# Last query group in two halves, and one operand's transposing loads held back until another has landed, in a two-attention kernel

## The chip, the cores and the metric

The kernel runs on one core of a Trainium2 chip. The metric is the device time of one execution in microseconds (us). Most executions of one kernel agree within 0.3%; an execution more than 1.5% above the fastest of its kernel counts as slow and is left out of the ratios. A profile is one further look at an execution: its span runs from the first to the last instruction and is some 2 us shorter than the device time. TensorE's granted clock is given as a share of full speed.

## The reference, cut to what matters

Two attentions, A and B, read two inputs of 2048 rows by 448 columns, and their outputs stand side by side.

```python
# A: 16 query heads of 28 columns share one key and one value head, full softmax
q = (x @ wq) as 16 heads;  k = x @ wk;  v = x @ wv
p = softmax(q k^T * 28 ** -0.5);  outA = (p v, heads joined) @ wo
# B: 16 heads; each query sees 8 keys at distances 0, 2, .. 14
q, k, v = x @ wqkv;  attn = softmax(q . k[pos - 2 w] * 28 ** -0.5, masked where pos < 2 w)
outB = (sum_w attn * v[pos - 2 w]) @ wo
```

A's scores are 16 heads x 2048 x 2048 exponentials, and they set the time. B is laid between them.

## The kernel before

A Python generator registers operations, each with what it reads (`R`), what it writes (`W`), an estimated duration and a priority `pr`. A scheduler derives the waits and lays all operations in one fixed order per engine. On the chip each engine then works through its own order: an operation that waits holds up everything behind it.

The loads. `xst` is a staging tile for A's first 512 rows; TensorE transposes them. All other rows come by transposing loads on SyncE's queue, A's (`xT_A`, 12 loads) and B's (`xT_B`, 16).

```python
a("act", 0.5, one(lambda e: e.dma_start(out=g.xst[:, :, :], in_=g.A_x[0, 0:512, :]...)),
  W=["xst"], dsem="i_xa0", land=3.2, pr=-21)
...
a("sp", 1.05, one(lambda e, c=c, t=t: e.dma_start(out=g.xT_A[...], in_=g.A_x[...], transpose=True)),
  R=["xst"], W=[("xT", c, t)], ..., pr=-20 + c)          # R is used here as "not before this has landed"
...
a("sp", 1.05, one(lambda e, c=c, t=t: e.dma_start(out=g.xT_B[...], in_=g.B_x[...], transpose=True)),
  W=[("xT_B", c, t)], ..., pr=-16 + c)
...
a("gp", 1.5, ..., W=["wqv"], dsem="i_wbv", land=5, pr=-7, ninc=2)   # B's value weights, GpSimd's queue
...
a("sp", 0.6, one(lambda e: e.dma_start(out=g.v_dram[0:PAD, :], in_=g.Vst[0:PAD, 0, :])),
  R=[("Vst", 0)], W=[("vd", -1)], dsem="i_vz", ..., pr=3, rel=4)     # 14 rows of zeros, end of the queue
```

B's first product. VectorE multiplies queries and keys of B into a tile that lies in the same memory as `xst` (the profile calls both `stage`), so the first block has to wait for everyone who still reads `xst`:

```python
op = a("dve", t_dve_2x(1024), ..., W=[("prodT", t)], pr=pr, rel=T)
if k == 0:
    op.deps.update(g.s.rd.get("xst", ()))     # all registered readers of xst
```

The score loop takes 512 queries of one of four head groups at a time ("group", 16 in all). In it ScalarE takes exponentials of three or two banks at once, VectorE takes 4 or 6 single banks of a group and none of the first (`OFF_AT`), and TensorE accumulates P times V in one bank. The last group's result is transposed and normalised in two column halves, one after the other, after the last exponential (`hv = 2`).

## Time and profile before

| before | |
|---|---|
| median of 3 runs | 461.0 us (460.56 to 461.21) |
| span of the profiled run | 459.2 us |
| to the first exponential / first start to last start / last end to end | 11.29 / 439.67 / 7.48 us |
| last `xT_B` load landed | 42.6 us |
| first multiply of B started | 53.1 us |

The middle number is start to start, so it leaves out the last exponential itself (0.76 us here).

### The profile page before, as it was taken

What the parts mean: (1) busy time and instruction counts of PE and PEld (TensorE: products, weight loads), DVE (VectorE), ACT (ScalarE), POOL (GpSimd) and SP (SyncE); (2) the same over time, 40 slices, a digit from 0 to 9 for tenths busy, and PEclk for the clock granted to TensorE, in tenths of its full rate; (3) what the DMA queues carried; (4) which work ended last, traced back from release to release, by engine and by line L of the source; (5) the groups of instructions that cost most, each with busy time, mean ns of one, the idle gap of its engine ahead of it and who ended that gap; (6) DMA issues with size and microseconds to landing.
All of it is one profiled execution on the core that took longest, in us unless ns stands there. A gap on an engine that the chain in (4) does not pass through costs nothing.

```text
span 459.2 us, 8717 instructions
## 1 busy us (share of the span) xinstructions
PE 427.7 (93%) x3682; PEld 163.6 (36%) x3682; DVE 380.7 (83%) x622; ACT 444.9 (97%) x430; POOL 9.4 (2%) x29
## 2 busy tenths in 40 slices
PE   8999999999999989999899999899899998989997
PEld 3333232323533324234353342224244342325343
DVE  6556889988798898989688889998988969889883
ACT  3999999999999999999999999999999999999994
POOL 7000000000000000000000000000000000000000
PEclk9999999999999999999999999999999999999999
DMA  7774303002201002020220120002022221214001
GB/s 152 128 162 95 109 27 100 1 1 90 92 15 40 19 10 82 20 81 22 81 91 30 44 83 18 0 13 92 0 97 92 70 78 30 72 31 142 10 1 61
DMA packets 42102, 27.34 MB, mean 60 GB/s; under 512 B 17474, under 2 KB 41904, under 8 KB 42064
## 3 DMA queue, kind: packets, MB, share of 16 engines
q1 hardware_dynamic: 40464, 25.28, 19.6%
q0 software_dynamic: 304, 0.73, 0.6%
q10 hardware_dynamic: 1296, 0.79, 0.5%
q8 instruction: 29, 0.48, 0.4%
q14 instruction: 9, 0.07, 0.1%
HBM read 17.60 MB, written 5.52 MB: 50 GB/s over the span
## 4 chain that ended last, share of the span: by engine, by line
ACT 86%; PE 11%; DVE 1%; DMA 1%; issue 0%
ACT expT L806 85%; PE ps L789 2%; PE ps L1079 2%; PE ps L850 2%; PE ps L787 1%; DMA stage<-in_A_x_dram 1%; PE ps L978 1%; PE ps L1086 1%; PE ps L937 1%; ACT e_t L1054 0%; PE ps L654 0%; PE ps L738 0%; PE ps L1028 0%; PE ps L434 0%; PE ps L993 0%
## 5 line engine op out<-in xcount | busy, mean ns | idle before, releaser
L806 ACT ACTIVATE expT<-ps 128x1024 bf16<-128x1024 f32 (+1 forms) x410 | 438.8, 1209 | 2.1 <-PE ps L789 1.9
L789 PE MATMUL ps<-qT,kT 32*128 32x512 bf16 x824 | 122.3, 385 | 11.6 <-ACT expT L806 9.3
L850 PE MATMUL ps<-expT,v_aug 128*32 128x512 bf16 x958 | 94.8, 389 | 1.0 <-ACT expT L806 1.0
L787 PE MATMUL ps<-qT,kz 128*128 128x512 bf16 x200 | 59.6, 383 | 9.9 <-ACT expT L806 9.4
L789 PEld LDWEIGHTS ps<-qT,kT 32*128 32x128 bf16 x824 | 30.1, 91 | 91.7 <-ACT expT L806 68.4
L883 DVE TENSOR_SCALAR d_x<-ps 128x512 f32<-128x512 f32 x66 | 45.4, 688 | 17.9 <-PE ps L789 16.8
L850 PEld LDWEIGHTS ps<-expT,v_aug 128*32 128x32 bf16 x958 | 24.3, 93 | 62.0 <-issue 55.4
L1073 DVE TENSOR_TENSOR prod<-Vsh,a_n 128x896 bf16<-128x896 bf16 x64 | 37.5, 614 | 7.9 <-PE ps L1079 7.9
L1019 DVE TENSOR_TENSOR stage<-qTB,kTB 112x1024 bf16<-112x1024 bf16 x64 | 42.3, 674 | 1.8 <-PE ps L1028 1.7
L1079 PE MATMUL ps<-ident,prod 128*112 128x128 bf16 x512 | 41.8, 224 | 0.0
L894 DVE SCALAR_TENSOR_TENSOR d_u<-d_u,d_x 128x1024 f32<-128x1024 f32 x33 | 40.1, 1215 | 0.1
L896 DVE SCALAR_TENSOR_TENSOR dexp<-d_u,d_x 128x1024 int16<-128x1024 f32 x33 | 40.0, 1213 | 0.1
L892 DVE SCALAR_TENSOR_TENSOR d_u<-d_x 128x1024 f32<-128x1024 uint16 x33 | 39.9, 1209 | 0.2
L1079 PEld LDWEIGHTS ps<-ident,prod 128*112 128x112 bf16 x512 | 34.2, 130 | 14.7 <-issue 10.9
L978 PE MATMUL ps<-xT_B,wqkv 128*128 128x512 bf16 x128 | 38.9, 383 | 0.0
L787 PEld LDWEIGHTS ps<-qT,kz 128*128 128x128 bf16 x200 | 12.2, 97 | 31.1 <-ACT expT L806 28.9
L1028 PEld LDWEIGHTS ps<-ones,stage 112*128 112x128 bf16 x512 | 18.5, 96 | 7.8 <-issue 4.8
L1028 PE MATMUL ps<-ones,stage 112*128 112x4 bf16 x512 | 21.2, 167 | 0.0
L738 PE MATMUL ps<-xT_A,wq 128*128 128x512 bf16 x64 | 19.8, 384 | 0.1
L1086 PE MATMUL ps<-wo_B,oT 112*128 112x448 bf16 x64 | 18.1, 357 | 0.0
L993 PE MATMUL ps<-wqv,xT_B 128*128 128x448 bf16 x64 | 17.5, 356 | 0.0
L913 DVE STREAM_TRANSPOSE PV_T<-ps 128x512 f32<-128x512 f32 (+1 forms) x17 | 11.4, 676 | 6.7 <-PE ps L850 6.5
(103 smaller groups left out, 303.3 us busy)
## 6 DMA issues: line engine op xcount, KB each, us to landing
Vsh<-v_scratch SPq DMA_DIRECT2D x16, 896.0 KB, 4.6
v_scratch<-Vst SPq DMA_DIRECT2D x16, 112.0 KB, 1.7
out_dram<-outB SPq DMA_DIRECT2D x16, 112.0 KB, 1.7
out_dram<-outA SPq DMA_DIRECT2D x14, 112.0 KB, 1.7
wqkv<-in_B_wqkv_dram SPq DMA_DIRECT2D x1, 672.0 KB, 5.4
stage<-in_A_x_dram ACTq DMA_DIRECT2D x1, 448.0 KB, 4.0
wo_B<-in_B_wo_dram SPq DMA_DIRECT2D x4, 98.0 KB
wo<-in_A_wo_dram SPq DMA_DIRECT2D x4, 98.0 KB
```

The costliest lines, as they stand in the source:

```text
L787: r = e.matmul(g.bank(b0 + i), g.kz[:, j, 128 * tb:128 * tb + 128], g.qT[:, sc % 2, t, :], start=True, stop=True)
L789: r = e.matmul(g.bank(b0 + i), g.kT[32 * j:32 * j + 32, 128 * tb:128 * tb + 128], g.qT[32 * j:32 * j + 32, sc % 2, t, :], start=True, stop ...
L806: x = a("act", t_exp(w), lambda e, b0=b0, w=w, n=n: e.activation(g.expT[:, n % ERING, 0:w], g.ps[:, 512 * b0:512 * b0 + w], ACT.Exp, scale ...
L850: x = e.matmul(g.bank(PVBANK, p0=32 * j, p1=32 * j + 32), g.v_aug[:, w, tb, :], src, start=first, stop=last, tile_position=(0, 32 * j))
L883: o = a("dve", t_dve_ps(512), lambda e: e.tensor_scalar(out=xx[:, 512 * h:512 * h + 512], in0=g.bank(bank), scalar1=-128.0 * A2, scalar2=1 ...
L892: a("dve", t_dve_1x(1024), lambda e: e.scalar_tensor_tensor(out=u, in0=lo, scalar=EP * F, in1=lo, op0=ALU.add, op1=ALU.mult), R=di, W=["d_ ...
L894: a("dve", t_dve_1x(1024), lambda e: e.scalar_tensor_tensor(out=v, in0=u, scalar=EQ * F * F, in1=lo, op0=ALU.add, op1=ALU.mult), R=["d_u"] ...
L896: a("dve", t_dve_1x(1024), lambda e: e.scalar_tensor_tensor(out=out, in0=v, scalar=EL / F ** 3, in1=xx, op0=ALU.mult, op1=ALU.subtract), R ...
L978: a("pe", t_mm(512), lambda e, u=u, t=t, kt=kt, w=w: e.matmul(g.bank(u.bank), g.wqkv[:, kt, w * D + KC * t:w * D + KC * t + 128], g.xT_B[: ...
L1019: op = a("dve", t_dve_2x(1024), lambda e, t=t, qv=qv, kv=kv: e.tensor_tensor(out=g.prodT[0:KC, t, :, :], in0=qv, in1=kv, op=ALU.mult), R=R ...
L1028: r = e.matmul(g.bank(u.bank, 128).rearrange("p (h w) -> p h w", w=WIN)[:, 4 * t:4 * t + 4, w], g.prodT[0:KC, t, w, :], g.ones4[:, :], sta ...
L1079: a("pe", 0.056, lambda e, u=u, t=t, w=w: e.matmul(g.bank(u.bank, 128, 128 * t, p1=KC), g.prod2[:, w, KC * t:KC * t + KC], g.ident[:, :], ...
```

## The change

Its intent: the last group is worked in two halves of 256 queries, so that the first half is normalised and projected while the second is still being scored, and only half remains after the last exponential. B's transposing loads wait for A's first rows, so that these land alone. Two warming matmuls are added. Six score banks on VectorE in three groups, which the change's label also names, are in the kernel before as well. Not shown below: the second half evicts no bank to VectorE, some priorities of A's projections change, and the scheduler charges for one more kind of mode switch on TensorE. These too can move the static order. The core of the diff, with cuts:

```diff
-TAILB = (0, 1, 2, 4)
-WARM = 7
+TAILB = (4, 0)
+WARM = 9
 OFF_AT.update({q: (0, 2, 3, 5, 7, 8) for q in (5, 9, 13)})
+OFF_AT[15] = (0, 2, 3, 5)
...
-  ... in_=g.B_x[...], transpose=True)), W=[("xT_B", c, t)], dsem=f"i_xb{c}.{t}", land=4.5, pr=-16 + c)
+  ... in_=g.B_x[...], transpose=True)), R=["xst"], W=[("xT_B", c, t)], dsem=f"i_xb{c}.{t}", land=4.5, pr=-16 + c)
...
+    def parts(self, u):
+        if u[:2] == (3, 3):       # last group: two key blocks of 256 queries in one bank
+            return [(2 * (u[2] % 8) + i, 256 * (u[2] // 8), 256) for i in range(2)]
+        return [(u[2], 0, 512)]
...
-    def a_quad_end(self, sc, t):
+    def a_quad_end(self, sc, t, hf=None):     # called once for each half of the last group
-        hv = 2 if last else 1
-        for hf in range(hv):
...
-        for s4 in range(4):
+        for s4 in range(4) if hf is None else (2 * hf, 2 * hf + 1):
```

More of the change, by code (lines that the diff above doesn't have):

```diff
@@ L284, in run @@
                     o.dense += 512 * o.fill
-                if o.tiled and not mode:
+                if o.tiled and (not mode or o.fill):
                     o.dur += self.MODE
@@ L609, in loads @@
                     out=g.xT_B[:, t, 512 * c:512 * c + 512], in_=g.B_x[0, 512 * c:512 * c + 512, XB0[t]:XB0[t] + 128],
-                    transpose=True)), W=[("xT_B", c, t)], dsem=f"i_xb{c}.{t}", land=4.5, pr=-16 + c)
+                    transpose=True)), R=["xst"], W=[("xT_B", c, t)], dsem=f"i_xb{c}.{t}", land=4.5, pr=-16 + c)
         a("sp", 1.2, lambda e: [
@@ L758, in a_q, with key @@
               R=["qadd"], W=[("qT", par, t)], use=u, pr=pr if first else -1)
+    def key(self, u):
+        return (3, 3, u[2] // 8) if u[:2] == (3, 3) else u[:2]
+    def parts(self, u):
+        if u[:2] == (3, 3):
+            return [(2 * (u[2] % 8) + i, 256 * (u[2] // 8), 256) for i in range(2)]
+        return [(u[2], 0, 512)]
     def a_loop(self):
@@ L764, in a_loop @@
         g.last_exp, g.pvs, g.evacs = {}, {}, []
-        quads = {(sc, t): [[] for _ in range(4)] for sc in range(4) for t in range(4)}
+        quads = {g.key(u): [[] for _ in range(4)] for u in units}
         dqs = {k: [[] for _ in range(4)] for k in quads}
@@ L784, in qk @@
                     e.matmul(g.bank(b0), g.warm[:, 0:128], g.warm[:, :], start=True, stop=True)
-                for i, (sc, t, tb, j) in enumerate(us):
-                    if box[0].full:
-                        r = e.matmul(g.bank(b0 + i), g.kz[:, j, 128 * tb:128 * tb + 128], g.qT[:, sc % 2, t, :], start=True, stop=True)
-                        continue
-                    r = e.matmul(g.bank(b0 + i), g.kT[32 * j:32 * j + 32, 128 * tb:128 * tb + 128],
-                                 g.qT[32 * j:32 * j + 32, sc % 2, t, :], start=True, stop=True, tile_position=(32 * j, 0))
+                for i, u in enumerate(us):
+                    sc, t, _, j = u
+                    for k, (tb, q0, nq) in enumerate(g.parts(u)):
+                        if box[0].full:
+                            r = e.matmul(g.bank(b0 + i, nq, nq * k), g.kz[:, j, 128 * tb:128 * tb + 128],
+                                         g.qT[:, sc % 2, t, q0:q0 + nq], start=True, stop=True)
+                            continue
+                        r = e.matmul(g.bank(b0 + i, nq, nq * k), g.kT[32 * j:32 * j + 32, 128 * tb:128 * tb + 128],
+                                     g.qT[32 * j:32 * j + 32, sc % 2, t, q0:q0 + nq], start=True, stop=True, tile_position=(32 * j, 0))
                 return r
             box = []
-            o = a("pe", 0.315, lambda e, qk=qk, box=box: qk(e, box=box), R=[("kT", tb // 4) for (_, _, tb, _) in us] + [("qT", sc % 2, t) for (sc, t, _, _) in us],
+            o = a("pe", 0.315, lambda e, qk=qk, box=box: qk(e, box=box), R=sorted({("kT", y[0] // 4) for u in us for y in g.parts(u)}) + [("qT", sc % 2, t) for (sc, t, _, _) in us],
                   W=[("ring", slot)], pr=-50)
@@ L797, in a_loop @@
             o.full = len(us) if len(us) > 1 else 0
-            o.opt = {x for (_, _, tb, _) in us for x in g.kz_ops[tb // 4]}
+            o.opt = {x for u in us for y in g.parts(u) for x in g.kz_ops[y[0] // 4]}
             o.fill = 0
@@ L811, in a_loop @@
                 g.last_exp[b0 + i] = x
-                quads[us[i][:2]][us[i][3]].append((us[i], ("expT", n % ERING), g.expT[:, n % ERING, 512 * i:512 * i + 512], 0))
+                quads[g.key(us[i])][us[i][3]].append((us[i], ("expT", n % ERING), g.expT[:, n % ERING, 512 * i:512 * i + 512], 0))
             if off:
@@ L819, in a_loop @@
                 for x in late.pop(0)[1]:
-                    qd = x[0][:2]
+                    qd = g.key(x[0])
                     g.nq[qd] = g.nq.get(qd, 0) + 1
@@ L831, in a_loop @@
             for u in us:
-                js = quads[u[:2]]
+                js = quads[g.key(u)]
                 while all(js):
                     g.pv_group([x.pop(0) for x in js])
-                if u[2:] == (15, 3):
+                if u[2:] == (15, 3) or u == (3, 3, 7, 3):
                     left = [x.pop(0) for x in js if x]
@@ L841, in pv_group @@
         g, a = self, self.s.add
-        qd = grp[0][0][:2]
+        qd = g.key(grp[0][0])
         all_pv = g.pvs.setdefault(qd, [])
@@ L846, in pv @@
         def pv(e):
-            for (_, _, tb, j), _, src, w in grp:
+            runs = [(y, k) + z for y in grp for k, z in enumerate(g.parts(y[0]))]
+            runs.sort(key=lambda x: x[1])
+            for ((_, _, _, j), _, src, w), k, tb, q0, nq in runs:
                 order = [o.seq for o, js in all_pv if j in js]
-                first, last = box[0].seq == min(order), box[0].seq == max(order)
-                x = e.matmul(g.bank(PVBANK, p0=32 * j, p1=32 * j + 32), g.v_aug[:, w, tb, :], src,
+                first, last = box[0].seq == min(order) and k == 0, box[0].seq == max(order) and (k + 1) * nq == 512
+                x = e.matmul(g.bank(PVBANK, nq, q0, p0=32 * j, p1=32 * j + 32), g.v_aug[:, w, tb, :], src[:, nq * k:nq * k + nq],
                              start=first, stop=last, tile_position=(0, 32 * j))
             return x
-        o = a("pe", 0.315, pv, R=sorted({y[1] for y in grp}) + sorted(
-            {(k, y[3], y[0][2] // 4) for k in ("v_aug", "v_aug1") for y in grp}), pr=-40, dense=700)
+        o = a("pe", 0.315 if len(qd) == 2 else 0.42, pv, R=sorted({y[1] for y in grp}) + sorted(
+            {(k, y[3], z[0] // 4) for k in ("v_aug", "v_aug1") for y in grp for z in g.parts(y[0])}), pr=-40, dense=700)
         o.tiled = o.pv = True
@@ L861, in pv_group @@
         g.npv[qd] = g.npv.get(qd, 0) + len(grp)
-        if g.npv[qd] == 64:
+        if g.npv[qd] == (64 if len(qd) == 2 else 32):
             g.a_quad_end(*qd)
@@ L867, in offload @@
         g = self
-        if n % 2 or us[0][:2] != us[-1][:2]:
+        if n % 2 or g.key(us[0]) != g.key(us[-1]):
             return 0
-        if us[0][:2] != g.quad:
-            g.quad, g.round = us[0][:2], n // 2
-        return int(n // 2 - g.round in OFF_AT.get(4 * us[0][0] + us[0][1], ()))
+        if g.key(us[0]) != g.quad:
+            g.quad, g.round = g.key(us[0]), n // 2
+        return int(n // 2 - g.round in OFF_AT.get(4 * us[0][0] + us[0][1], ()) and g.quad[2:] != (1,))
     def d_exp(self, bank, slot, sib):
@@ L899, in d_exp @@
         return ("dexp", m % DR), out[:, 512 * h:512 * h + 512].bitcast(BF16)
-    def a_quad_end(self, sc, t):
+    def a_quad_end(self, sc, t, hf=None):
         g, a = self, self.s.add
         end = 12.0 + QT * (4 * sc + t + 1)
-        last = sc == 3 and t == 3
-        evacs = []
-        hv = 2 if last else 1
-        for hf in range(hv):
-            w, b = 512 // hv, 16 // hv
-            cs, bs = slice(w * hf, w * hf + w), slice(b * hf, b * hf + b)
-            keys = [hf] if last else [0, 1]
-            kk = lambda n: [(n, t % 2, x) for x in keys]
-            p0 = -30 if last else -1
-            o = a("dve", t_dve_ps(w), lambda e, cs=cs: e.transpose(out=g.PV_T[:, t % 2, cs], in_=g.bank(PVBANK)[:, cs]),
-                  W=kk("PV"), pr=-30)
-            o.deps.update(x for x, _ in g.pvs[sc, t])
-            evacs.append(o)
-            pt = g.PV_T[:, t % 2, :].rearrange("p (b e) -> p b e", e=32)
-            a("dve", 0.25, lambda e, pt=pt, bs=bs: e.reciprocal(out=g.rden[:, t % 2, bs], in_=pt[:, bs, DH]),
-              R=kk("PV"), W=kk("rden"), pr=p0)
-            a("dve", t_dve_1x(w), lambda e, pt=pt, bs=bs: e.tensor_tensor(
-                out=g.oN[:, bs, :], in0=pt[:, bs, :], in1=g.rden[:, t % 2, bs].unsqueeze(2).to_broadcast([128, b, 32]), op=ALU.mult),
-              R=kk("PV") + kk("rden"), W=[("oN", x) for x in keys], pr=p0)
-            a("dve", 0.12 + 1.04e-3 * w, lambda e, cs=cs: e.transpose(
-                out=g.oTn[:, t, cs], in_=g.oN[:, :, :].rearrange("p b e -> p (b e)")[:, cs]),
-              R=[("oN", x) for x in keys], W=[("oTn", t, x) for x in keys], pr=p0)
-        g.evacs = evacs
-        pr = end + 20
@@ new lines, in a_quad_end @@
+        last = hf == 1
+        w, b, lo = (512, 16, 0) if hf is None else (256, 8, 256 * hf)
+        cs, bs = slice(lo, lo + w), slice(lo // 32, lo // 32 + b)
+        keys = [0, 1] if hf is None else [hf]
+        kk = lambda n: [(n, t % 2, x) for x in keys]
+        p0 = -30 if last else -1
+        o = a("dve", t_dve_ps(w), lambda e: e.transpose(out=g.PV_T[:, t % 2, cs], in_=g.bank(PVBANK)[:, cs]),
+              W=kk("PV"), pr=-30)
+        o.deps.update(x for x, _ in g.pvs[(sc, t) if hf is None else (sc, t, hf)])
@@ new lines, in a_quad_end @@
+        g.evacs = [o]
+        pt = g.PV_T[:, t % 2, :].rearrange("p (b e) -> p b e", e=32)
+        a("dve", 0.25, lambda e: e.reciprocal(out=g.rden[:, t % 2, bs], in_=pt[:, bs, DH]), R=kk("PV"), W=kk("rden"), pr=p0)
+        a("dve", t_dve_1x(w), lambda e: e.tensor_tensor(
+            out=g.oN[:, bs, :], in0=pt[:, bs, :], in1=g.rden[:, t % 2, bs].unsqueeze(2).to_broadcast([128, b, 32]), op=ALU.mult),
+          R=kk("PV") + kk("rden"), W=[("oN", x) for x in keys], pr=p0)
+        a("dve", 0.12 + 1.04e-3 * w, lambda e: e.transpose(
+            out=g.oTn[:, t, cs], in_=g.oN[:, :, :].rearrange("p b e -> p (b e)")[:, cs]),
+          R=[("oN", x) for x in keys], W=[("oTn", t, x) for x in keys], pr=p0)
@@ L928, in a_quad_end @@
         if t < 3:
             return
-        for s4 in range(4):
+        for s4 in range(4) if hf is None else (2 * hf, 2 * hf + 1):
             blk = 4 * sc + s4
+            pr = (end + 20 if hf is None else end) + s4
             if last:
-                u = Use(f"F{sc}.{s4}", (TAILB[s4],), late=True)
+                u = Use(f"F{sc}.{s4}", (TAILB[s4 - 2],), late=True)
+                pr = -30
             else:
@@ L938, in a_quad_end @@
                     g.bank(u.bank, D), g.oTn[:, tt, 128 * s4:128 * s4 + 128], g.wo4[:, tt, :], start=tt == 0, stop=tt == 3),
-                  R=[("oTn", tt, s4 // 2), "wo4"], W=[u], use=u, pr=pr + s4 + tt if not last else -30 + tt, dense=448)
+                  R=[("oTn", tt, s4 // 2), "wo4"], W=[u], use=u, pr=pr + tt, dense=448)
                 if last and tt == 0:
-                    o.deps.add(g.last_exp[TAILB[s4]])
+                    o.deps.add(g.last_exp[TAILB[s4 - 2]])
             ob = blk % 4
```

## The prediction

> **What bounds the kernel now.** I read the busy shares and the chain on the page first, then one table of three stretches (before, during and after ScalarE's exponentials), then the chain of waits at both ends and the timeline there.
>
> ```profile
> PE 427.7 (93%) x3682; PEld 163.6 (36%) x3682; DVE 380.7 (83%) x622; ACT 444.9 (97%) x430; POOL 9.4 (2%) x29
> ...
> ACT 86%; PE 11%; DVE 1%; DMA 1%; issue 0%
> ```
>
> ScalarE is busy 97% of the span and 86% of the last chain is its own. The table by stretch (columns: stretch, length, then busy time and count of each engine) shows where the other 3% are:
>
> ```profile
> 11.29:451.72 440.43, 414.40 (x3613) 157.71 (x3612) 369.28 (x588) 440.18 (x422) 0.80 (x4) 1.00 0.20 57
> 451.72:459.20 7.48, 4.27 (x30) 1.90 (x28) 4.57 (x12) 0.98 (x2) 0.00 (x0) 1.00 0.24 77
> 0.00:11.29 11.29, 9.07 (x42) 3.97 (x42) 6.86 (x23) 3.77 (x6) 8.58 (x25) 1.00 0.75 154
> ```
>
> So the span is three terms: 11.29 us until the first exponential, 440.43 us of exponentials in which ScalarE is busy for 440.18, and 7.48 us after the last one. Busy is not the same as tight, so I look for the floor of the middle term. By form, and on ScalarE's timeline near the end:
>
> ```profile
> L806 ACT ACTIVATE expT<-ps 128x1024 bf16<-128x1024 f32 x270 | 269.7, 1066 | 0.1
> L806 ACT ACTIVATE expT<-ps 128x1536 bf16<-128x1536 f32 x139 | 207.2, 1490 | 2.0 <-PE ps L789 1.9
> ```
> ```profile
> 445.16 6.56 ACT L806 ACTIVATE expT<-ps 128x1536 bf16<-128x1536 f32 x6
> ```
> ```profile
> 447.39 4.33 ACT L806 ACTIVATE expT<-ps 128x1536 bf16<-128x1536 f32 x4
> ```
>
> The last two lines are the same run of exponentials asked for in two windows: two fewer, and it starts 2.23 us later. One three-bank and one two-bank exponential thus take 2.23 us start to start, less than 1.490 + 1.066 because they overlap. The forms differ by 0.424 us, so a two-bank one costs (2.23 - 0.424) / 2 = 0.90 and a three-bank one 1.33. Floor: 139 x 1.33 + 270 x 0.90 + some 0.8 for the single-bank one = 429. The loop is 11 us above that; eight softmax exponentials of attention B at 0.3 to 0.4 each are about 3 of it, and the remaining 8 are spread over 410 steps as waits of hundredths of a us. There is no single wait to remove.
>
> The first stretch, from the chain (start, length, what) and the timeline:
>
> ```profile
> 0.81 4.02 DMA stage<-in_A_x_dram
> ...
> 4.88 1.89 PE ps L654 x16
> 6.76 0.64 PE ps L667 x2
> 7.41 0.88 PE ps L738 x4
> 8.31 0.60 ACT q_sq L744
> ```
> ```profile
> 1.25 3.17 PE L646 MATMUL ps<-warm 128*128 128x512 bf16 x7 [1.25 <-DVE warm L543]
> ...
> 1.94 3.86 SPq L608 DMA_TRANSPOSE xT_B<-in_B_x_dram  x3
> ...
> 5.84 16.61 SPq L603 DMA_TRANSPOSE xT_A<-in_A_x_dram  x12
> ```
>
> The load of the first x lands at 4.83 and from then TensorE is the path: 16 transposes, then K and Q matmuls one after another to about 8.3. Last, VectorE after the last exponential:
>
> ```profile
> 452.41 0.78 DVE L913 STREAM_TRANSPOSE PV_T<-ps 128x256 f32<-128x256 f32 x2 [5.22 <-PE ps L850]
> 453.11 0.32 DVE L918 RECIPROCAL rden<-PV_T 128x8 f32<-128x8 f32 x2
> 453.34 0.72 DVE L920 TENSOR_TENSOR oN<-PV_T,rden 128x256 bf16<-128x256 f32 x2
> 453.99 0.76 DVE L923 STREAM_TRANSPOSE oTn<-oN 128x256 bf16<-128x256 bf16 x2
> 454.67 0.65 DVE L1082 CAST oT<-ps 112x512 bf16<-112x512 f32 x1
> 455.25 1.14 DVE L947 CAST outA<-ps 128x448 bf16<-128x448 f32 x2
> 456.35 0.62 DVE L1089 CAST outB<-ps 128x448 bf16<-128x448 f32 x1
> ```
>
> VectorE works without a break from 452.41 to 456.97; the last store is issued at 457.00 and 2.2 us later the kernel is over.
>
> **What the Trainium skill says.** "ScalarE: Activation LUTs", section "What ACT_TABLE_LOAD costs": an activation with immediate operands is 186 ns + 0.833 ns per column and back-to-back ones overlap by some 93 ns. That gives 1.04 and 1.47 us; the trace has 1.066 and 1.490, with a larger overlap of (1.066 + 1.490 - 2.23) / 2 = 0.16. Nothing in the change alters the columns, so the floor stays. "TensorE: Matmul & The Clock Gate", Part 1: a cold array runs 512 columns in 427 ns and 128 in 107, a warm one in 216 and 56, and it warms after a busy window of about 3.4 us whose phase isn't tied to the kernel's start. The trace agrees: seven warming matmuls are busy for 3.17 us with a mean of 630 ns (6 x 0.427 + 0.61), and 16 transposes take 1.89, while the four Q matmuls (0.88) are warm. The same page, Part 3, lets row-tiled matmuls overlap only on different row groups; here three score matmuls with 32 rows start within 10 ns of each other at 10.85 and end within 0.41 us. "DMA: Bandwidth & Descriptors", "Anatomy of one DMA": about 2 us of a transfer are fixed and the semaphore waits until the last byte is confirmed; the x load of 448 KB takes 4.02.
>
> **The change part by part.** The label also names the three groups with six offloaded banks; groups 5, 9 and 13 have them before as well, so that part changes nothing. The built orders confirm it: 410 exponentials of the same forms and 66 banks on VectorE in both.
>
> (1) Transposing loads of B's x wait for A's first x. The DMA view of the first 6 us shows 262, 347, 363, 382, 373, 375, 376, 375 and 265 GB/s in the 0.15 us slices from 3.0: 468 KB, where x alone is 459. The three transposing loads took 4.7 us to land and move their bytes after x has passed, so they took little from it. I give this 0.1 us. A's own transposing loads start at about 4.9 instead of 5.84, which helps chunks needed later, but ScalarE shows no wait for them now, so 0.
>
> (2) Two more warming matmuls. In the built order they don't stand in front of the transposes; one stands between the transposes and the first K matmul, one between that and Q, while one K matmul moves behind Q. TensorE is the path there (the chain is unbroken from 4.88 to 8.3), so Q comes one matmul later: 0.22 if warm, up to 0.43 if cold. I take +0.25. Sum of (1) and (2): +0.15, first exponential at 11.4 to 11.5.
>
> (3) The scheduler's charge for a mode switch after a fill, with the changed offload rounds of the last group, shuffles the static order. Fills inside score groups go from 12 to 9. The 8 us of small waits are redrawn rather than removed: 0, give or take 0.8.
>
> (4) The last group in halves: per score bank two matmuls of 256 columns for one of 512, and PV likewise (matmuls 3,684 to 3,805). ScalarE and VectorE see the same columns. On TensorE a dense pair costs the same, but two halves of one bank share a row group, so I expect three tiled banks to take 4 x 0.107 = 0.43 instead of 0.215: +0.21 us before a three-bank exponential, +0.11 before a tiled two-bank one. Before a two-bank exponential ends (0.90) TensorE must see the bank free (0.16), issue (0.43) and drain (0.17): 0.76 plus a handover of 0.05, so it just fits unless other work stands in front. About 13 such steps, a few late by 0.05 to 0.2: +0.4.
>
> (5) The tail. It loses one of each pair of half-width steps: about 0.36 + 0.15 + 0.36 + 0.36 = 1.2 us of VectorE. But in the built order block 14's outB (0.62) now stands between reciprocal and normalisation, and all 32 transposing matmuls of B's block 15 stand behind the last PV; before, 22 of them were done earlier. TensorE after the last PV (issued until 0.56 after the last exponential): one output projection 0.19, two of B's block 14 0.38, 32 x 0.056 = 1.79, six projections 1.13, four of B's block 15 0.76, which reaches 4.81, plus 0.16 to drain, 0.05 to hand over, outB 0.62: 5.6 to 5.7 after the last exponential, where it is 456.97 - 451.72 = 5.25 now. So +0.4: the bound of the tail changes from VectorE to TensorE and the halves gain nothing.
>
> Sum: 0.15 + 0 + 0.4 + 0.4 = about +0.9.
>
> **The rivals.** (a) The tail gains: if TensorE gets through B's last block earlier, only VectorE's shorter chain remains and 1.2 - 0.62 = 0.6 us comes off, for 460.4. For it: the halves were made for this. Against it: the 32 matmuls stand behind the last PV in program order. (b) The hold matters more: were x to land 0.5 us sooner, with TensorE warm by the transposes (16 x 0.05 = 0.8 less), the start would shorten by about 1 us: 460. Against it: the near-full bandwidth, and a clock that warms by a free-running window. (c) The halves overlap worse than I assume, each late step costing 0.2: 26 x 0.2 = 5 us, 466. Against it: 0.59 us of the 2.23 of a pair is slack in front of most two-bank steps. (d) A changed order stalls TensorE on B's x, which now arrives about 3 us later: the first of it is wanted at 38.0 and should land near 32, so no.
>
> **Range and chances.** My sum says 461.9; tuning usually keeps what measured better, and (a) and (b) both pull down, so I set 461.3, with 459.8 to 462.7 as the range. Two per cent is 9.2 us, more than both ends together could give and far over any sum above: within 2% has a chance of 0.98, the other two 0.01 each.
>
> **What would show it.** First exponential at 11.3 to 11.6 (b says 10.3 to 10.7). First to last exponential 440 to 441.5 (c says over 443). Last exponential to end of span 7.6 to 8.0, with the chain through L1091, L949 and L1098 on TensorE (a says under 7.0, through VectorE). Exponentials' mean durations unchanged. I am wrong if the middle stretch moves by more than 1.5 us, which would mean that order in the loop is worth more than I could see.

## More of the kernel before

The multiply on before's timeline (start, length, what):

```profile
53.08 0.68 DVE L1019 TENSOR_TENSOR stage<-qTB,kTB 112x1024 bf16<-112x1024 bf16 x1
```

## The result, and the profile after

| | median | range | runs |
|---|---|---|---|
| before | 461.0 us | 460.56 to 461.34 | 6 |
| after | 464.78 us | 464.17 to 466.17 | 6 |

The ratio is 1.0088, with a 95% interval of 1.0072 to 1.0104: clearly slower, though within 2%, and outside the predicted range. Here and below (with one exception, told under the table of experiments) a ratio is the mean time of one kernel's fast runs over that of the other's fast runs of the same rounds, so it is not quite the ratio of the medians.

The same table by stretch for the kernel after (stretch, length, then busy time and count of TensorE, its weight loads, VectorE, ScalarE, GpSimd; granted clock, DMA share, GB/s):

```profile
0.00:10.41 10.41, 8.26 (x43) 3.15 (x43) 6.55 (x23) 3.77 (x7) 8.58 (x25) 1.00 0.51 118
10.41:454.41 444.00, 407.43 (x3653) 158.12 (x3707) 370.13 (x592) 440.24 (x422) 0.80 (x4) 1.00 0.21 58
454.41:462.20 7.79, 4.99 (x55) 3.13 (x53) 4.41 (x9) 0.54 (x1) 0.00 (x0) 0.98 0.23 76
```

The start is 0.9 us shorter and the tail 0.3 longer, but the loop is 3.6 us longer while ScalarE is busy for the same 440.2 us. So ScalarE stood still in the loop. On the page, the chain and one group say where (for the group: count, busy time and mean ns, then idle time before it and its releaser):

```profile
ACT 78%; PE 11%; SPq 8%; DMA 1%; DVE 1%; issue 0%; DVEq 0%
...
L1031 DVE TENSOR_TENSOR stage<-qTB,kTB 112x1024 bf16<-112x1024 bf16 x64 | 42.0, 676 | 4.1 <-DMA xT_B<-in_B_x_dram 2.9
```

ScalarE's share of the last chain fell from 86 to 78%, and SyncE's queue, absent from the chain of before, holds 8% of it: the first 45 us of the path are now loads. The stretch from 40 to 53 us, before and then after:

```profile
40.00:53.00 13.00, 11.86 (x84) 3.25 (x77) 11.55 (x17) 13.00 (x14) 0.00 (x0) 1.00 0.34 85
```
```profile
40.00:53.00 13.00, 10.05 (x56) 2.62 (x56) 8.10 (x13) 9.49 (x10) 0.00 (x0) 0.87 0.46 105
```

ScalarE loses 3.5 of 13 us, nearly the whole loss of the loop. The chain of waits and the timeline there (start, length, what; in brackets the idle time before and what ended it):

```profile
41.36 1.27 SPq L609
...
42.67 2.76 DMA xT_B<-in_B_x_dram
...
45.51 0.69 DVE stage L1031
...
47.51 0.61 DVE d_x L899
...
48.25 0.38 PE ps L795
```
```profile
45.51 0.69 DVE L1031 TENSOR_TENSOR stage<-qTB,kTB 112x1024 bf16<-112x1024 bf16 x1 [2.89 <-DMA xT_B<-in_B_x_dram]
48.25 0.38 PE L795 MATMUL ps<-warm 128*128 128x512 bf16 x1 [2.90 <-DVE d_x L899]
49.00 2.52 ACT L820 ACTIVATE expT<-ps 128x1536 bf16<-128x1536 f32 x2 [2.25 <-PE ps L803]
```

VectorE's first multiply of B waits 2.89 us for the last of B's 16 loads. Behind it in VectorE's order stand the eviction `d_x`, which frees a score bank, and more; so TensorE waits 2.90 us and ScalarE 2.25. This multiply needs only the first 512 rows of B, whose four loads had landed by 30.1 us. It waits for the last load because `R=["xst"]`, meant as "not before x has landed", also registers each of the 16 loads as a reader of the staging tile, and the multiply waits for all its readers. The wait is untrue: no load of B touches the tile.

A second gap of ScalarE (1.16 us, before the exponential at 52.68) follows at the lower clock. "TensorE: Matmul & The Clock Gate", section "HAM oscillation — how this bites in real kernels", says that a wait for data which crosses the activity window makes TensorE throttle and the next work start cold. The trace agrees but for the moment: after 2.9 idle us the granted clock is 0.50 from 48.95 to 52.35 us (0.87 over the whole stretch, where it was 1.00), but the first matmul after the wait, at 48.25, still took 0.38 us; the half clock began 0.7 us after the work did.

Two things made this wait bite, and they come from different parts of the change. One is the load queue (SyncE's timeline, for which the prediction has the lines of before):

```profile
4.78 16.19 SPq L604 DMA_TRANSPOSE xT_A<-in_A_x_dram  x12
```

Before, SyncE issued three of B's loads from 1.94 to 5.80 us, while x was under way. Held, it issues nothing in that time, and the whole in-order queue behind ends 2.8 us later: the last `xT_B` landed at 45.4, not 42.6 us. The other is VectorE's order: the multiply that stood at 53.1 us now stands at 42.6, just ahead of the late load.

### The profile page after: what moved, and what is told of

Same layout as the page of the kernel before. It is cut to its first block, busy times and chain, and to the rows that moved or that the text cites. A ratio compares the mean times of both kernels' runs of the same rounds, so it can differ in the third digit from the quotient of the medians.

```text
span 462.2 us, 8915 instructions
## 1 busy us (share of the span) xinstructions
PE 420.7 (91%) x3748; PEld 164.4 (36%) x3803; DVE 381.1 (82%) x623; ACT 444.5 (96%) x429; POOL 9.4 (2%) x29
## 4 chain that ended last, share of the span: by engine, by line
ACT 78%; PE 11%; SPq 8%; DMA 1%; DVE 1%; issue 0%; DVEq 0%
ACT expT L820 78%; SPq L609 4%; SPq L604 3%; PE ps L1091 2%; PE ps L803 2%; PE ps L866 2%; PE ps L800 1%; PE ps L949 1%; DMA stage<-in_A_x_dram 1%; PE ps L1098 1%; DMA xT_B<-in_B_x_dram 1%; ACT e_t L1066 1%; PE ps L1040 0%; DVE d_x L899 0%; PE ps L1005 0%
## 5 line engine op out<-in xcount | busy, mean ns | idle before, releaser
L803 PE MATMUL ps<-qT,kT 32*128 32x512 bf16 (+1 forms) x848 | 118.7, 373 | 13.3 <-ACT expT L820 10.2
L866 PE MATMUL ps<-expT,v_aug 128*32 128x512 bf16 (+1 forms) x1018 | 95.6, 378 | 1.0 <-DVE v_aug L718 0.5
L800 PE MATMUL ps<-qT,kz 128*128 128x512 bf16 (+1 forms) x210 | 59.5, 364 | 13.7 <-ACT expT L820 11.3
L899 DVE TENSOR_SCALAR d_x<-ps 128x512 f32<-128x512 f32 x66 | 45.4, 687 | 18.7 <-PE ps L803 17.0
L1091 PE MATMUL ps<-ident,prod 128*112 128x128 bf16 x512 | 42.9, 224 | 0.3 <-DVE qT L757 0.3
L1091 PEld LDWEIGHTS ps<-ident,prod 128*112 128x112 bf16 x512 | 34.4, 129 | 15.8 <-issue 12.9
L990 PE MATMUL ps<-xT_B,wqkv 128*128 128x512 bf16 x118 | 36.9, 384 | 0.8 <-issue 0.5
L800 PEld LDWEIGHTS ps<-qT,kz 128*128 128x128 bf16 x240 | 15.5, 97 | 31.4 <-ACT expT L820 28.1
L739 PE MATMUL ps<-xT_A,wq 128*128 128x512 bf16 x61 | 18.6, 382 | 0.4 <-issue 0.3
L1098 PE MATMUL ps<-wo_B,oT 112*128 112x448 bf16 x64 | 17.9, 357 | 0.0
L757 DVE TENSOR_SCALAR qT<-ps,cols 128x512 bf16<-128x512 f32 x16 | 11.9, 747 | 6.7 <-PE ps L753 6.7
```

What stands on the lines that cost most here:

```text
L800: r = e.matmul(g.bank(b0 + i, nq, nq * k), g.kz[:, j, 128 * tb:128 * tb + 128], g.qT[:, sc % 2, t, q0:q0 + nq], start=True, stop=True)
L803: r = e.matmul(g.bank(b0 + i, nq, nq * k), g.kT[32 * j:32 * j + 32, 128 * tb:128 * tb + 128], g.qT[32 * j:32 * j + 32, sc % 2, t, q0:q0 + ...
L866: x = e.matmul(g.bank(PVBANK, nq, q0, p0=32 * j, p1=32 * j + 32), g.v_aug[:, w, tb, :], src[:, nq * k:nq * k + nq], start=first, stop=last ...
L899: o = a("dve", t_dve_ps(512), lambda e: e.tensor_scalar(out=xx[:, 512 * h:512 * h + 512], in0=g.bank(bank), scalar1=-128.0 * A2, scalar2=1 ...
L1091: a("pe", 0.056, lambda e, u=u, t=t, w=w: e.matmul(g.bank(u.bank, 128, 128 * t, p1=KC), g.prod2[:, w, KC * t:KC * t + KC], g.ident[:, :], ...
```

## The experiments

Fifteen kernels ran in four calls, each call with its own runs of the kernel before. The calls ran on four different chips, so runs of different calls are compared by their ratio to before. All results are correct but one, told below.

| run | what it is | median (range) of fast runs, us | ratio to before, 95% |
|---|---|---|---|
| after | the change | 464.78 (464.17–466.17) | 1.0088 [1.0072, 1.0104] |
| e2 | before + hold | 461.61 (460.55–463.86) | 1.0026 [0.9997, 1.0054] |
| e3 | after, no hold | 461.93 (461.78–461.94) | 1.0025 [1.0010, 1.0040] |
| e5 | after, no untrue wait | 465.6 (463.13–467.95) | 1.0107 [1.0060, 1.0153] |
| e6 | after, multiply later in the order | 466.42 (464.88–467.0) | 1.0118 [1.0098, 1.0139] |
| e7 | e5 + zero store early | 463.74 (460.54–465.07) | 1.0049 [1.0009, 1.0089] |
| e8 | after + zero store early | 464.95 (464.04–465.47), 1 slow | 1.0137 [1.0065, 1.0209], see below |
| f1 | e7 + value weights late | 461.09 (460.38–462.39) | 1.0010 [0.9996, 1.0024] |
| f4 | after + value weights late | 464.34 (463.67–465.13), 2 slow | 1.0080 [1.0065, 1.0096] |
| f3 | e2 + value weights late | 460.3 (460.13–460.95) | 0.9998 [0.9984, 1.0011] |
| e9 | e3, other tail (wrong result) | 459.49 (459.3–459.68) | does not count |
| e10 | before, other tail order | 460.98 (460.5–461.24) | 0.9998 [0.9983, 1.0013] |
| g2 | e3, evictions earlier | 462.43 (462.03–462.93) | 1.0034 [1.0022, 1.0046] |
| g3 | e3, TensorE order | 461.38 (461.19–464.93) | 1.0028 [1.0004, 1.0051] |
| f2 | e3, both | 460.27 (460.06–460.44) | 0.9991 [0.9978, 1.0003] |
| g1 | f1 + f2's tail | 460.6 (459.99–462.59) | 0.9998 [0.9983, 1.0013] |

The medians of before were 460.71 (e2 to e6), 461.0 (e7 to e10), 460.63 (f) and 460.98 (g). The ratio of e8 takes in its slow run of 471.54; its three fast runs alone have a mean of 464.82 us, 1.0083 of before's. What made the slow runs of e8 and f4 slow is not known.

### Is it the hold, or the order?

Theory 1: the untrue wait costs the 3 us. Rivals: the hold by itself, or the new order by itself. Four kernels take these apart.

e2 puts the hold into the kernel before:

```diff
-  ... transpose=True)), W=[("xT_B", c, t)], ...
+  ... transpose=True)), R=["xst"], W=[("xT_B", c, t)], ...
```

> The kernel before with the hold alone. Its built order keeps the first multiply of B some 10 us later (behind the fourth 512-column eviction of the exponentials on VectorE), so the same untrue wait should be over before it is reached. Theory 1: no stall, 460 to 461.3. Rival (holding B's loads starves the loop by itself): 463 to 465. On the start: if the hold is what let TensorE be warm at its transposes, the first exponential comes at 10.4; if that is the phase of the clock's window, it may be 10.4 or 11.3 in any kernel.

e3 takes it out of the kernel after (the reverse edit).

> The changed kernel without the hold. Theory 1: no reader is added, so no stall: 461.0 to 462 (the longer tail of 0.3 stays). If the hold made the early start, the first exponential is back at 11.3 to 11.6 and the time near 461.6; if two more warming matmuls or the clock's phase made it, it stays near 10.4 and the time near 460.7. Rival (halves and order): 464.

e5 leaves the hold and the order, instruction for instruction, and drops the untrue waits of the multiply alone:

```diff
-op.deps.update(g.s.rd.get("xst", ()))
+op.deps.update(x for x in g.s.rd.get("xst", ()) if not (x.dsem or "").startswith("i_xb"))
```

> The changed kernel with the first multiply of attention B no longer made to wait for B's own transposing loads; the built order of every engine is the same instruction for instruction. Theory 1 (the hold entered B's loads as readers of the staging tile that this multiply overwrites, so VectorE stands still until the last of them lands): no idle of VectorE before that multiply, no gap of over 1 us between exponentials, first to last exponential about 439.7 us instead of 443.3, and the time falls by about 3.7 to 461.1 (460.4 to 461.8). Rival (the halves and the new order cost it, the wait is covered anyway): 464 or more, with the same 443 us of loop.

e6 keeps the wait and moves the first multiply back to where it stood before, by an earliest time 30 us later:

```diff
-... W=[("prodT", t)], pr=pr, rel=T)
+... W=[("prodT", t)], pr=pr, rel=T + (30.0 if k == 0 else 0.0))
```

> The changed kernel with hold and untrue wait kept, but the first multiply released 30 us later in the schedule, so that it stands behind 53 us in the order. Theory 1 with position (the wait costs only because the multiply stands early in VectorE's fixed order): no stall, 460.4 to 461.8. Rival (the wait costs wherever it stands): 463 to 465.

In e3 the loss of 3 us is gone: its loop is 439.49 us, as before, and every run lies within 0.2 us. So the hold is needed for the loss. e2 mostly did without the loss too (461.61 us, between the two forecasts), so the hold is not enough: in the order of before, the multiply stands late. e3's multiply starts at 43.25 us, early as in the kernel after. It has no wait for the late loads, since without `R=["xst"]` they are no readers of the tile.

But theory 1 fell with e5: the wait is gone and the time is not better. e6, forecast at 460.4 to 461.8, was slower still. VectorE's and ScalarE's timeline in e5:

```profile
51.73 0.62 DVE L1009 CAST Vst<-ps 128x448 bf16<-128x448 f32 x1 [2.00 <-DMA v_scratch<-Vst]
...
53.39 1.02 ACT L820 ACTIVATE expT<-ps 128x1024 bf16<-128x1024 f32 x1 [1.24 <-PE ps L803]
```

VectorE passes the multiply at 43.43 us without a wait, arrives at the eviction of B's first values six us later and waits 2.00 us there, for the store of zero rows. That wait is true (the store reads the same `Vst` slot) and its store is the last in the same late queue: issued at 48.76 us, where before issued it at 46.46. From the 35th to the 43rd exponential e5 falls from 0.8 to 4.8 us behind before, with a granted clock of 0.50 from 53.9 to 60.7 us. e6 waits at the same place, for 2.61 us. In e3, with the new order and no hold, the same eviction already waits 0.40 us, without a gap in ScalarE; in the old order with hold it waits 0.68 us in e2, also without one.

### Two waits on one queue

Theory 2: the hold makes the whole queue late, VectorE meets it twice, and removing one wait only uncovers the other. e7 removes both: e5's edit, and the zero store ahead of B's loads in the queue. On the other four engines the order is unchanged. e8 moves the store and keeps the untrue wait.

```diff
-R=[("Vst", 0)], W=[("vd", -1)], dsem="i_vz", land=2.5, pr=3, rel=4)
+R=[("Vst", 0)], W=[("vd", -1)], dsem="i_vz", land=2.5, pr=-16.7)
```

> The changed kernel with two edits: the first multiply of B no longer lists B's 16 loads as readers to wait for, and the tiny store of zero rows stands ahead of B's loads in the SyncE queue, not behind them. Order on TensorE, VectorE, ScalarE and GpSimd is the changed kernel's, instruction for instruction. Theory (the hold delays the whole in-order load queue by some 2.8 us, and two waits in VectorE's order, one untrue on the last xT_B load and one true on the zero-rows store, each turn that delay into a stall): neither VectorE wait is there, no gap of ScalarE above 0.5 us between 40 and 62 us, first to last exponential 439.3 to 440.5 us, median 460.8 to 462.2, that is what the changed kernel without the hold took (461.9) give or take half a microsecond. Rival (the new VectorE order, or a colder TensorE, costs the 3 us by itself, and the waits only show where): still 464 or more.

> The changed kernel with the zero-rows store early and the untrue wait kept. Theory: the first multiply of B still waits 2.7 to 3.5 us for the last xT_B load near 45 us (the queue is another 0.4 us later), ScalarE loses 2.4 to 4 us there, median 463.5 to 465.5. Rival (only the store at the end of the queue costs): 461 to 462.2.

The profiled run of e7 is what theory 2 says: 460.54 us, loop 439.26, no gap, and neither VectorE operation waits for a load, though the last `xT_B` landed at 45.8:

```profile
42.74 0.65 DVE L1031 TENSOR_TENSOR stage<-qTB,kTB 112x1024 bf16<-112x1024 bf16 x1
49.32 0.62 DVE L1009 CAST Vst<-ps 128x448 bf16<-128x448 f32 x1 [0.28 <-PE ps L1005]
```

The other three runs of e7 took 463.3 to 465.1 at clocks of 0.992 to 0.996, so its median missed the forecast, and something still stalls in some executions. e8 shows what. Its profiled run lost its time elsewhere than I expected: not at 45 us but at the start of the loop. Stretch 12 to 20 us, e7 and then e8, and TensorE in e8:

```profile
12.00:20.00 8.00, 7.38 (x62) 2.45 (x61) 5.10 (x14) 8.00 (x10) 0.20 (x1) 1.00 0.80 156
```
```profile
12.00:20.00 8.00, 5.97 (x33) 1.69 (x33) 2.92 (x9) 5.82 (x6) 0.20 (x1) 0.68 0.83 144
```
```profile
13.43 0.39 PE L668 MATMUL ps<-xT_A,wk 128*128 128x512 bf16 x1 [0.77 <-DMA xT_A<-in_A_x_dram]
...
15.52 0.61 PE L668 MATMUL ps<-xT_A,wk 128*128 128x512 bf16 x1 [1.26 <-DMA xT_A<-in_A_x_dram]
```

The key matmuls of A's second 512 rows wait for A's own third and fourth transposing loads; ScalarE is busy for 5.82 of 8 us, and the clock falls to 0.68. After that the compute runs 3.7 us behind e7's, and so the multiply, at 46.46, comes just after the last load (46.38). A stall at any of three places gives the delay back to the loads, and the others then hide. e6's profile had this one too.

The fourth `xT_A` load was issued about 1.1 us earlier with the hold than without it, yet it landed at 14.1, 14.1, 14.4, 15.0, 15.5 and 16.3 us in the six profiles with hold so far (after, e7, e2, e5, e8, e6), against 14.1 to 15.0 in the seven profiles without it (before, e3, e9, e10, f2, g2, g3). So the earlier issue brought nothing, and two of the six landed later than any without hold. These two, e8 and e6, are the ones that stalled.

### The third place: the start

Theory 3: with the hold, A's loads run into GpSimd's two loads of B's value weights, issued from 8.9 us on. "DMA: Bandwidth & Descriptors", section "Queues, rings and completion order", says that each DMA engine takes turns between the queue rows that have work for it, packet by packet; so a large load from another queue delays the ones beside it. No run here shows the turns themselves, but the runs below show the delay. The edit holds these two loads until the fourth `xT_A` load has landed. No engine's order changes.

```diff
-W=["wqv"], dsem="i_wbv", land=5, pr=-7, ninc=2)
+R=[("xT", 1, 3)], W=["wqv"], dsem="i_wbv", land=5, pr=-7, ninc=2)
```

f1 is e7 with it, f4 is the kernel after with it, f3 is e2 with it.

> The run with both VectorE waits gone, and in addition GpSimd's two loads of B's value weights (issued at 8.9 and 9.7 us so far) wait until the fourth xT_A load of key chunk 1 has landed; every engine's order is the same, instruction for instruction. Theory (with the hold the xT_A loads of chunk 1 run into these two large loads in the DMA queues; the fourth of them landed at 14.1 to 16.3 us in the five profiles with hold, and above 15 us TensorE and ScalarE stop for 3 us, which is the spread of 460.5 to 465.1 in the run without this edit): the fourth load lands by 13.5 us, no gap of ScalarE over 0.5 us between 12 and 62 us, and all times lie within 1.2 us of each other, median 460.3 to 461.9. Rival (the spread comes from TensorE's clock, not from the load): still a run above 463, median above 462.5.

> The changed kernel with nothing but the value-weight loads held back until the fourth xT_A load has landed. Theory: the start can no longer stall, so the untrue wait of the first multiply must show in full: 2.7 to 3.5 us near 43 to 46 us in the profile, times within 1.5 us of each other, median 463.5 to 465. Rival (the start is where the changed kernel loses): 460.5 to 462.

> The kernel before with the hold and with the value-weight loads held back. The kernel before with the hold alone ran 460.55 to 463.86. Theory: with the collision gone the times draw together, 460.2 to 461.2, median 460.4 to 460.9, the same as before or up to 0.5 us better; no wait over 1 us of VectorE on a load. Rival: still a run above 462.5.

The fourth load landed at 12.7, 12.4 and 12.6 us in the three (13.9 in g1, told below), where it landed at 14.1 or later in all profiles without the edit, and none stalls at the start. So the two large loads do delay it. They are issued at 8.9 us without the hold as well, and the edit was not tried there: that the collision comes from the hold is not shown. f1 is down to 461.09 us; four of its five runs lie within 0.8 us and one took 462.39 at a clock of 0.996, so a remnant stays. f3, against e2, comes down from 461.61 to 460.3, its range from 3.3 to 0.8 us; its VectorE still waits 1.34 us for the zero store, and in this old order ScalarE has no gap of 0.5 us from it. f4 is the control: with the start safe, the untrue wait shows in full, in the line below, and its fast runs take 464.34 us. Each of the three effects has now been seen to stall a run by itself: the untrue wait in f4, the zero store in e5, the start in e8.

```profile
45.76 0.69 DVE L1031 TENSOR_TENSOR stage<-qTB,kTB 112x1024 bf16<-112x1024 bf16 x1 [3.30 <-DMA xT_B<-in_B_x_dram]
```

### The tail

e3 is free of the hold and still 1.2 us behind before. Its loop is level; its time from the last exponential to the end is 8.50 us against 7.48. Two edits were tried: B's last two blocks get priority on TensorE, and the last group's evictions move to other rounds. e9 does both, with the evictions on before's rounds; e10 gives the priority to the kernel before.

```diff
-..., use=u, pr=pr, dense=...)                          # both TensorE steps of B's output
+..., use=u, pr=-45 if k >= 14 else pr, dense=...)      # e9, e10; in f2, g1 and g3: -35
...
-OFF_AT[15] = (0, 2, 3, 5)
+                                                       # e9: the line removed; in f2, g1 and g2: (0, 1, 2, 3)
```

> The changed kernel without the hold, with the TensorE work of B's last two blocks (their transposing matmuls and their output projection) set ahead of the second half's, and the last head group's VectorE evictions back on rounds 0, 2, 5, 7. Theory for the tail: with B's 32 transposing matmuls out of the way, the end is the second half's own chain (256-wide transpose, reciprocal, multiply, transpose, two projections), last exponential's end to end 6.2 to 6.9 us against 7.5 of before and 8.5 of the changed kernel without hold; median 459.6 to 460.6. Rival (TensorE's place in the tail is not what binds, the halves gain nothing in any order): tail 7.4 or more, median 461.3 or more.

> The kernel before (no halves, no hold) with the same priority for the TensorE work of B's last two blocks. If the halves are what shortens the tail in the other run: VectorE's two-halves chain of four 512-wide-in-pieces steps binds here, tail 7.1 to 7.5, median 460.3 to 461.2, and the difference to the other run is 0.5 to 1.2 us. If the placing of B's last block alone is the gain: both runs the same within 0.3 us.

e9's output is wrong (not a number), and its 459.49 us is the time of a kernel that leaves work out: as the code reads, a half has fewer rounds than a group, so its round 7 never comes, the bank evicted in round 5 waits for a partner, and the first half is never closed. The profile has 14 copies of A's output blocks where there should be 16. e10 gains nothing in time. In its one profile the tail is shorter, 7.17 us, and the loop longer, 440.38 against 439.67, so the priority by itself moved time rather than saved it.

f2 repeats e9 with evictions in rounds that exist, and does all the work. g2 and g3 then split it, the evictions alone and the priority alone.

> The changed kernel without the hold, with the last head group's evictions in rounds 0, 1, 2, 3, not 0, 2, 3, 5, and B's last two blocks set ahead of the halves' projections on TensorE. All the work is done, which the run that came out wrong did not do (it never closed the first half, so its two blocks of output were not computed). If the order of the tail's TensorE work is what costs the changed kernel its 1.2 us in the tail: last exponential's end to end 7.3 to 7.9 against 8.5 without this, median 460.6 to 461.4. If the tail is bound by the total work left after the last exponential: 8.2 or more and 461.6 or more.

> The changed kernel without the hold, with the last head group's evictions in rounds 0, 1, 2, 3 alone. If the late evictions hold up VectorE's multiplies of B's last block and so the 32 transposing matmuls: median 460.3 to 461.0. If the place of those matmuls in TensorE's order is what counts: nothing gained or lost, 461.6 to 462.3.

> The changed kernel without the hold, with the priority of B's last two blocks on TensorE alone. If the place of the 32 transposing matmuls is what counts: 460.3 to 461.0, last exponential's end to end 7.5 to 7.9 us. If they cannot go earlier because VectorE's multiplies, behind the evictions, come too late: 461.5 to 462.1 and 8.3 to 8.6 us, and only both edits together gain.

Tails in the profiles: e3 8.50, g2 9.32, g3 8.19, f2 7.32 us. Earlier evictions alone are worse (462.43 us, above both forecasts), the priority alone gains 0.3 us, both together gain 1.2. That fits the reading that TensorE's transposing matmuls can only go earlier if the order asks for it and VectorE, freed of late evictions, has their input ready; the reading itself was not tested further. In none of the valid kernels did the halves beat before's tail by more than 0.15 us, and the shortest valid tail, 7.17 us, is e10's, which has no halves. The chain of waits in the tail of the kernel after, then of f2:

```profile
455.72 1.79 PE ps L1091 x32
457.51 1.13 PE ps L949 x6
458.64 0.77 PE ps L1098 x4
...
459.44 0.62 DVE outB L1101
```
```profile
451.86 1.80 PE ps L1091 x32
...
455.44 0.59 DVE outB L1101
```

Even in f2 the 32 transposing matmuls of B's last block stand whole after the last exponential (450.86).

g1 has everything: the hold without its three effects, and f2's tail.

> The changed kernel with the hold kept but its three side effects gone (untrue wait dropped, zero-rows store early, value weights held back until the fourth xT_A load has landed), and the tail of the run that came out at 0.9991 of before. If the hold by itself is worth nothing: the same as that run, 460.0 to 460.7, ratio 0.998 to 1.001. If TensorE's earlier start with the hold counts for the 0.5 to 0.9 us that the first exponential has sometimes come earlier: ratio 0.996 to 0.998. If its delayed queue still costs somewhere: above 461, and a wait on a load in the profile.

Five of its six runs take 459.99 to 461.01 us, and the profiled one 462.59: there the value weights, now issued at 14.2 us, met the loads of A's third 512 rows, and TensorE waited 1.62 us for one that landed at 20.59 (18.0 in f1). So in this execution, as the profile reads, holding these loads moved the collision and did not abolish it. The hold itself is worth nothing that shows: g1 has 0.9998, f2 without hold 0.9991, f3 0.9998. f2 is the best kernel and mends the change, but its interval includes 1: no version is shown to beat the kernel before.

## Why the prediction was right or wrong

The class, within 2%, was right. The time, 461.3 us with a range to 462.7, was wrong by 3.5 us, and the sum of 461.9 by 2.9.

**The step that failed** is rival (d): "A changed order stalls TensorE on B's x, which now arrives about 3 us later: the first of it is wanted at 38.0 and should land near 32, so no." The 3 us were right (2.8) and the first of it did come in time (it landed by 30.1 us, and TensorE first used it at 36.9). But I asked only for the engine that uses the data and only for the first load. The first to stop was VectorE, 2.89 us at the *last* load, of whose data it needs nothing at that point, by an untrue wait that the hold created. With that gone it stopped 2.00 us (e5) at a true wait, for a small store at the end of the same queue. And A's own loads, set to 0 in step (1), held TensorE for 0.77 and 1.26 us at the start in e8. None of the three is in the sum; in the kernel after, the first made the loop 3.6 us longer. The hold was priced as a bandwidth question (0.1 us), while what it cost was place in an in-order queue.

**Start, (1) and (2).** Predicted 11.4 to 11.5, measured 10.41. One half of rival (b) came true, the 16 transposes ran warm (1.07 us, where before took 1.89), and that is nearly all of the 0.88 us; the other half did not, x landed only 0.07 us sooner. But the same start code gave 11.01 and 11.27 in e5 and e6, before's code with the old `WARM` and hold 10.63 in e2, and f1 11.44. The first exponential moves by 1 us between profiles of like starts, so I credit this neither to the hold nor to the warming matmuls. What makes the transposes run warm in one execution and cold in another was not tested.

**Order, (3).** 0 give or take 0.8 holds for the order without the hold: loops of 439.49 (e3) and 439.21 (f2) against 439.67. What the order cost was not in small waits but in room to wait: a late zero store made VectorE wait 1.34 us in the old order (f3) without a gap, and 2.00 us in the new one (e5) with a gap of 1.24.

**Halves in the loop, (4).** Predicted +0.4; the same loops show nothing. The loop has room for the doubled matmuls.

**Tail, (5).** The mechanism held: the bound moves to TensorE, through L1091, L949 and L1098, and 7.79 us falls in the 7.6 to 8.0 named. The size of +0.4 was right for the kernel after and too small for the same tail without the hold: +1.02. There four matmuls of B's block 14 (0.76 us), not two, stand ahead of the 32, and two projections of A stand before the last four of these.

My own test, "wrong if the middle stretch moves by more than 1.5 us", caught the error: it moved by 3.6. Its reading, that the order is worth more than I could see, was half of it: order mattered, but through a late queue.

Open: what stalls in one run of f1 (462.39 us) and one of g3 (464.93, and without the hold), which were not profiled; and why the scheduler brought the multiply forward by 10 us, and which part of the change did it (the halves, the warming matmuls or the charge for a mode switch), since no run takes these apart.

## What to carry to other kernels

A dependency used as a delay has two ends: look up who waits for the *readers* of the tile before you register sixteen new ones, and price a held load by everything behind it in its in-order queue, down to the smallest store. When removing a wait brings no time, look for the next one on the same late resource before you give up the theory. And an order whose loop time is level (439.49 us in e3) can still have used up its slack, so that a delay elsewhere becomes a stall.

## What the Trainium skill lacked or had wrong

- "DMA: Bandwidth & Descriptors" gives transposing loads a bandwidth; for the cost on the issuing queue it has only a cycle count for small tiles, in its part on another chip. Here a 512 x 128 load mostly holds SyncE for 1.26 us and the next follows 1.30 us after it (as at 5.84 and 7.14 us in before), and the 28 of them take 38 us of queue (3.86 + 16.61 + 17.51). The kernel's own estimate was 1.05.
- The same page has no time from the issue of such a load to its landing, and "VectorE: DVE Perf Modes" has only one figure for a 128 x 128 tile. Here it is 2.7 to 3.0 us for the last load of B (42.67 to 45.43 in the kernel after) and for the fourth load of A from 3.8 (8.55 to 12.39 in f4, the value weights held back) to 7.4 us (8.88 to 16.30 in e6, beside them).
- "ScalarE: Activation LUTs", section "What ACT_TABLE_LOAD costs", has back-to-back activations overlap by some 93 ns. In before, exponentials of 1024 and 1536 columns that follow one another start 904 and 1330 ns apart in the median, 135 ns less than the page's 186 ns + 0.833 ns per column. The prediction's 160 ns set mean durations of the whole run against one pair of starts; its 0.90 and 1.33 us per exponential stand.
